# Expert products of an FNet + PEER block: all sixteen groups in seven part products, a seventh pair, sums kept or made in the expert stage

## Chip, core and metric

The kernel runs on one core of a Trainium2 chip. The core's engines work from queues of their own, in the order of the program: PE (matmuls), DVE (elementwise, one-hot building), ACT (activations, copies), POOL (elementwise), and SP, which here issues the DMAs. The metric is the device time of one execution in microseconds (us). Before the change it is 1130.89 us, the median of three runs (1129.87 to 1134.87).

## The reference

x is 1 x 2048 x 512. The output is x plus two branches of its layer norm xn: a Fourier mix (real part of a DFT over both axes) and a mixture of 4096 tiny experts.

```python
q = einsum("nd,dhc->nhc", xf, w_q)              # 32 heads, two halves of 128
s1, s2 = q1 @ k1.T, q2 @ k2.T                   # 64 keys each
# top 2 of each half, 4 candidates, top 2 of them: top_s, top_e (of 4096)
g = softmax(top_s, axis=-1)
act = gelu(einsum("nd,nhkd->nhk", xf, u[top_e]))
out_B = einsum("nhk,nhk,nhkd->nd", g, act, v[top_e])
return x + fnet(xn) + out_B
```

## The kernel before

**Stages.** Up to 431 us the kernel makes the layer norm, the folded DFT, the query scores (`s_mm`, L252), their top 2 and the routing numbers. Beside that it loads u and v and splits each into an upper and a lower f16 part (`fill_uv`, L772). From 431 us on runs the expert stage, with the 2048 tokens as 16 tiles of 128. It computes all 4096 experts for each token instead of gathering them.

**The expert stage, per token tile b.**
- z: u times x for all experts, in 16 groups of 256 experts, each product as three f16 matmuls (upper·upper, upper·lower, lower·upper), then gelu on ACT into the tile's `act`.
- g: `g_mm` (L1235) makes, for 32 tokens, a matrix of the routing weights over all experts. DVE builds one-hot matrices L (128x2048, L1246) and R (128x512, L1251, times the weight in L1254), 16 tokens at a time, in three rotating L/R buffers, and PE multiplies them into one of two PSUM buffers. Four g_mm make a tile: G(b,0) to G(b,3).
- w: `w_part` (L1259) multiplies `act` by g on DVE (L1264) and splits it into f16 parts: ACT copies the upper (L1271), DVE subtracts for the lower (L1272).
- v: `v_part` (L1294), eight v steps of twelve 512-column matmuls each, sums w times v in a PSUM bank.
- `add_x` (L1309) adds x to the Fourier rows on POOL (L1314); `finish` (L1316) adds the v sum on DVE (L1318) and stores.

**Pairs.** Tiles 2 to 13 go in six pairs through `z_pair` (L1175). For three sets of four groups (QUADS: groups 4 to 15) it uses seven part products on 128-column halves instead of eight, by a Strassen-Winograd scheme: operations 1 to 7, each 24 matmuls of 128 columns (L1168). Operations 1, 2 and 4 read blocks of u, 3, 5, 6 and 7 sums of u; 4, 5, 6 and 7 read sums of x. DVE adds the parts up (L1204, L1212, L1216) with copies on ACT between. The sums of u lie in HBM (`s_d`), made in the score stage by `sum_u` (L800), and come on chip through three rotating places (`ring_load`, L1148), four per quad and pair. The sums of x for the pair lie in HBM too (`t_d`), made in the score stage by `sum_x` (L817) on POOL and ACT, and are loaded in one 512 KB transfer (`x4`). Groups 0 to 3 go as four plain steps of 24 matmuls of 256 columns (`u_part`, L1082). The order within a pair is a list, where c is a plain step and the letter after an operation names the quad:

```python
SEQ = "1a 5a 2a 6a c 3a 1b 7a 2b 5b 4a 6b c 3b 1c 7b 2c 5c 4b 6c c 3c 7c c 4c".split()
```

Tiles 0, 1, 14 and 15 go alone, through plain steps with 128 columns.

**The order of the work.** It is written out by hand: a list of phases and a plan, which hangs pieces of work on a step number (cg) of a phase.

```python
phases = [("z", 0), ("z", 1), ("v", 0)]
for b in range(2, 14, 2):
    phases += [("z", b, b + 1), ("v", b - 1), ("v", b)]
phases += [("z", 14), ("v", 13), ("z", 15), ("v", 14), ("v", 15)]
```

So a cycle is a pair, then the v phase of the last tile of the pair before, then that of the new pair's first tile. G(b,0) and G(b,1) of a pair's first tile stand within the pair (cg 9 and 12 of 16), all its w parts in the v phase behind it, and there also G and W of the second tile, whose last g_mm, G(b+1,3), stands at the start of the next pair. Into free places the plan puts U units (`compare`, L1323: a check of the DFT tables, its operands cx come by DMA, DVE folds them in L1351 and L1357) and F units (`fit`). A scheduler may move an instruction ahead of others on its engine, but each engine's queue is then fixed.

Of the kernel before, what the change touches and what calls it, by code (L numbers as in the profile page):

```python
# [31 lines left out]
QUADS = (8, 10, 12, 14), (9, 11, 13, 15), (4, 5, 6, 7)  # L32
PAIRS = tuple(range(2, 14, 2))
# [3 lines left out]
def tile_fnet_peer(ctx, tc, x, ca, cb, c5, wt, wf, wr, wq, kt, ut, vn, out):  # L37
# [17 lines left out]
    t_d = dram.tile([NT // 2, P, 4 * D], F16, name="t_d")  # L55
# [665 lines left out]
    def part_b(safe, stS, stP, stQ, stE, xt, u_sb, cmp_p, w4):  # L721
# [50 lines left out]
        def fill_uv(which, g, at=None):  # L772
# [10 lines left out]
            if which == 0 and not safe and any(g in q for q in QUADS):  # L783
                SRAW[g] = raw
                sum_u(g, 0)
# [14 lines left out]
        def sum_u(g, part, at=None):  # L800

            qd, t = next((n, q.index(g)) for n, q in enumerate(QUADS) if g in q)
            par = [f for w, f in fills if w == 0 and any(f in q for q in QUADS)].index(g) % 2
# [12 lines left out]

        def sum_x(b, part, at=None):  # L817

            n = (0, 2, 4, 4, 7, 5)[PAIRS.index(b)]
            f, t4 = scratch(n), scratch(n + 1)  # L820
            if part == 0:
                v = xq[b // 2]
                nc.gpsimd.tensor_copy(f[:, 0:1], behind(one, at))
                nc.gpsimd.tensor_tensor(f.rearrange("p (q f) -> p q f", q=2),  # L824
                                        v[:, :, 0].rearrange("p q k n -> p q (k n)"),
                                        v[:, :, 1].rearrange("p q k n -> p q (k n)"), op=ALU.add)
                b11, b21, b12, b22 = [f[:, k * 256:k * 256 + 256] for k in range(4)]
                r = [t4[:, k * 256:k * 256 + 256] for k in range(4)]
                nc.gpsimd.tensor_tensor(r[0], b12, b11, op=ALU.subtract)
                nc.gpsimd.tensor_tensor(r[1], b22, r[0], op=ALU.subtract)  # L830
                nc.gpsimd.tensor_tensor(r[2], b22, b12, op=ALU.subtract)
                nc.gpsimd.tensor_tensor(r[3], b21, r[1], op=ALU.subtract)
                return
            split4(part - 1, t4, f.bitcast(F16)[:, 0:2 * D],
                   lambda i: t_d[b // 2, :, i * 2 * D:i * 2 * D + 2 * D], at)
# [158 lines left out]
        for (which, g), n in zip(fills, slots):  # L994
            todo[n].append(lambda at, w=which, g=g: fill_uv(w, g, at))
            todo[n - (3 if n < 119 else 1)].append(lambda at, w=which, g=g: fill_load(w, g))
            if which == 0 and not safe and any(g in q for q in QUADS):
                todo[n + 5].append(lambda at, g=g: (sum_u(g, 1, at), sum_u(g, 2)))
        if not safe:
            for n, b in zip((19, 22, 25, 106, 109, 118), PAIRS):  # L1000
# [521 lines left out]
        def G(b, k):  # L1522
            return lambda: g_mm(b, k)
# [249 lines left out]
```

## Time and profile before

| | |
|---|---|
| median of three runs | 1130.89 us |
| the profiled execution, its own time | 1132.17 us |
| its span, first to last instruction | 1130.4 us |
| busy: PE, DVE, ACT, POOL | 1114.2, 960.3, 657.5, 319.4 us |
| granted PE clock | 0.998 |

Some 1.8 us of the profiled execution's time lie around the span. Times in rows are microseconds from the span's start. A row of a timeline has the start, the duration, the engine, the line of the kernel, the operation, "output<-inputs", the tile's shape and how many instructions it stands for; behind it, in brackets, the idle time of the engine before it and what ended that. A row grouped by line has, behind the bar, the busy time in all and the mean of one in ns, then the idle time before. Matmuls overlap each other, so their durations exceed the distance between their starts.

### The profile page before, as it was taken

The page shows a single profiled execution, that of the slowest core. Times are in us where ns is not written, and L with a number is a line of the kernel's source. Part 1 is how long each engine was busy: PE and PEld are TensorE (multiplying, and loading weights), DVE is VectorE, ACT ScalarE, POOL GpSimd, SP SyncE. Part 2 cuts the span into 40 slices and gives each one's busy share as a digit, 9 for nine tenths or more (in the row PEclk, how much of TensorE's full clock was granted, in tenths as well). Part 3 has the DMA queues.
Part 4 walks back from the last instruction along what each step waited for, and adds up shares of the span by engine and source line. Part 5 has one row for each costly group of instructions (what it writes and reads, how often), then busy time and mean ns, then how long its engine had stood idle before and what let it go on. Part 6 is the DMA issues. An engine that isn't in the chain of part 4 may idle for free.

```text
span 1130.4 us, 28284 instructions
## 1 busy us (share of the span) xinstructions
PE 1114.2 (99%) x11180; PEld 724.4 (64%) x11180; DVE 960.3 (85%) x2873; ACT 657.5 (58%) x1099; POOL 319.4 (28%) x357
## 2 busy tenths in 40 slices
PE   9999999999999999999999999999999999999997
PEld 6455454544545459788588479479569569567763
DVE  7899979989889899976996896896998887889782
ACT  6557598798898465454446446445435535545552
POOL 1416896888889750000000000000010010000000
PEclk9999999999999999999999999999999999999999
DMA  9984455345353315464755755665656756575742
GB/s 274 289 207 171 162 168 197 112 154 190 105 187 103 104 50 190 157 249 143 258 216 184 239 206 199 235 218 187 226 199 215 227 199 225 190 246 167 239 150 106
DMA packets 122540, 213.10 MB, mean 189 GB/s; under 512 B 34580, under 2 KB 62107, under 8 KB 122398
## 3 DMA queue, kind: packets, MB, share of 16 engines
q1 hardware_dynamic: 122096, 211.13, 56.3%
q8 instruction: 89, 1.46, 0.5%
q14 instruction: 53, 0.43, 0.1%
q10 hardware_dynamic: 302, 0.08, 0.1%
HBM read 178.34 MB, written 27.07 MB: 182 GB/s over the span
## 4 chain that ended last, share of the span: by engine, by line
PE 50%; DVE 10%; DMA 3%; ACT 2%; POOL 2%; issue 1%; SPq 0%; DVEq 0%; ACTq 0%; POOLq 0%
PE v L1301 24%; PE z L1168 13%; PE z L1095 10%; PE g L1256 4%; DMA cx<-in_cb_dram 3%; DVE L L1246 2%; DVE vals L956 1%; DVE idx L960 1%; DVE w L1264 1%; DVE act L1272 1%; DVE cx L1351 1%; DVE R L1251 0%; DMA fit<-in_wq_dram 0%; DVE cx L1340 0%; POOL v L824 0%
## 5 line engine op out<-in xcount | busy, mean ns | idle before, releaser
L252 PE MATMUL s<-m,xq 128*128 128x512 f16 x1344 | 297.4, 379 | 1.0 <-ACT ss L952 0.5
L1301 PE MATMUL v<-v,act 128*128 128x512 f16 x1056 | 233.4, 379 | 1.0 <-DMA v<-v_d 1.0
L252 PEld LDWEIGHTS <-xq 128*128 128x128 f16 x1344 | 129.8, 98 | 152.2 <-issue 2.4
L1314 POOL TENSOR_TENSOR y<-y,xr 128x512 f32<-128x512 f32 x15 | 26.1, 1740 | 623.4 <-DMA y<-y_d 383.7
L1246 DVE TENSOR_TENSOR L<-io_lam,cmp 128x2048 f16<-128x2048 f16 x128 | 157.5, 1230 | 26.9 <-PE g L1256 26.8
L1301 PEld LDWEIGHTS <-act 128*128 128x128 f16 x1056 | 101.2, 98 | 118.7 <-issue 1.3
L1095 PE MATMUL z<-xb,u 128*128 128x128 f16 (+1 forms) x2112 | 154.3, 234 | 0.1
L1095 PEld LDWEIGHTS <-u 128*128 128x128 f16 x2112 | 141.4, 98 | 6.6 <-issue 0.2
L956 DVE MAX8 vals<-ss 128x8 f32<-128x64 f32 x896 | 133.5, 216 | 5.6 <-ACT ss L952 5.6
L1301 PE MATMUL v<-v,w 128*128 128x512 f16 x480 | 106.3, 379 | 0.1
L952 ACT ACTIVATE ss<-s,wsc 128x512 f32<-128x512 f32 x120 | 81.4, 682 | 41.2 <-PE s L252 35.1
L1377 ACT ACTIVATE cx<-cx 128x896 f32<-128x896 f32 x64 | 60.4, 944 | 72.6 <-DVE cx L1357 53.2
L1168 PEld LDWEIGHTS <-s 128*128 128x128 f16 x1656 | 94.8, 98 | 0.1
L960 DVE FIND_INDEX8 idx<-vals,ss 128x8 uint16<-128x256 f32 x224 | 93.8, 419 | 0.0
L1271 ACT ACTIVATE act<-w 128x1024 f16<-128x1024 f32 x36 | 48.3, 1357 | 68.3 <-DVE w L1264 68.0
L1301 PEld LDWEIGHTS <-w 128*128 128x128 f16 x480 | 45.9, 98 | 53.6 <-issue 0.4
L1168 PE MATMUL z<-x,s 128*128 128x128 f16 x1248 | 78.1, 219 | 0.0
L1168 PEld LDWEIGHTS <-u 128*128 128x128 f16 x1296 | 74.9, 98 | 1.8 <-issue 1.4
L1256 PEld LDWEIGHTS <-L 128*128 128x128 f16 x2048 | 60.3, 96 | 12.7 <-issue 2.1
L1351 DVE TENSOR_TENSOR cx<-cx 128x512 f32<-128x512 f32 (+2 forms) x84 | 48.4, 613 | 23.5 <-DMA cx<-in_cb_dram 23.5
L1264 DVE SCALAR_TENSOR_TENSOR w<-act,scl,g 128x1024 f32<-128x1024 f32 x44 | 55.8, 1277 | 10.3 <-ACT act L1195 10.3
L1256 PE MATMUL g<-R,L 128*128 128x32 f16 x2048 | 61.9, 176 | 1.6 <-DVE R L1254 1.5
(363 smaller groups left out, 1802.3 us busy)
## 6 DMA issues: line engine op xcount, KB each, us to landing
v<-v_d SPq DMA_DIRECT2D x67, 512.0 KB, 4.3
s<-s_d SPq DMA_DIRECT2D x59, 512.0 KB, 4.8
cx<-in_cb_dram SPq DMA_DIRECT2D x64, 448.0 KB, 4.7
w<-in_wq_dram SPq DMA_DIRECT2D x28, 512.0 KB, 6.0
fit<-in_wq_dram SPq DMA_DIRECT2D x28, 512.0 KB, 4.3
uv<-in_vn_dram SPq DMA_DIRECT2D x16, 512.0 KB, 3.5
uv<-in_ut_dram SPq DMA_DIRECT2D x16, 512.0 KB, 4.2
s_d<-v SPq DMA_DIRECT2D x24, 256.0 KB, 3.7
```

What stands on the lines that cost most here:

```text
L252: nc.tensor.matmul(ps, xt[i][:, l, kd, :], m[:, r, kd, :], start=(n == 0), stop=(n == 3 * KD - 1))
L952: nc.scalar.activation(s, ps, AF.Copy, scale=inv)
L956: nc.vector.max(vals[:, i, w, :, h], s[:, g, :])
L960: nc.vector.max_index(idx[:, i, w].rearrange("p k h -> p (k h)"), vals[:, i, w, 0:2].rearrange("p k h -> p (k h)"), s[:, w * HC:g + 1, :]. ...
L1095: nc.tensor.matmul(ps if n == 1 else ps.rearrange("p (b n) -> p b n", b=2), ug[:, l, c % 2, kd, :], xb2[:, k0, r, kd, :] if n == 1 else xb ...
L1168: nc.tensor.matmul(bank[:, t * P:(t + 1) * P], lt, rt, start=(t == k == 0 and op in "125"), stop=(t == 3 and k == 5), skip_group_check=op ...
L1246: nc.vector.tensor_tensor(L.rearrange("p t (l two) -> p t l two", two=2), io_lam.rearrange("p (l two) -> p l two", two=2).unsqueeze(1).to_ ...
L1256: nc.tensor.matmul(p[:, hf, t * NC:(t + 1) * NC], L[:, t, :], R[:, t, :], start=True, stop=True)
L1264: nc.vector.scalar_tensor_tensor(w, act[:, :, ts], fw, p.rearrange("p h (n c) -> p c (h n)", c=NC), op0=ALU.mult, op1=ALU.mult)
L1301: nc.tensor.matmul(pv, w16[:, c, :, l], v_sb[g][:, r, cc, :], start=(n + cc == 0 and k == 0), stop=(n == 15 and cc == 1 and k == 2))
L1351: nc.vector.tensor_tensor(v, v, tv[:, 0:1].to_broadcast([P, len(ix), 256]), op=o)
L1377: later.append(lambda: nc.scalar.activation(tf[:, P:], tf[:, P:], AF.Abs, accum_out=chk[:, n:n + 1]))
```

## The change

- **Quads:** groups 0 to 3 become a fourth quad, so a pair has 28 part products and no plain step. u sums for groups 0 to 3 (`u_sums`) are made on POOL and ACT late in the score stage.
- **A seventh pair:** tiles 14 and 15 go as a pair; the phases end pair (14,15), v 13, v 14, v 15.
- **Order in a pair:** a v step of the tile before (`v`) and both g_mm of the pair's first tile (`g`) stand at the end, before the last operation 4.
- **One u sum per group kept on chip:** `first_sum` loads the sum that operation 5 uses over a u block that nothing reads any more (once, in the first v phase). Three sums per quad still go through the rotating places, twelve per pair as before.
- **Sums of x in the expert stage:** `sum_x` and `t_d` are gone. `x_sums` makes them from the x tiles on POOL and ACT, in the v phase before the pair, with the buffer of an `act` tile as scratch.
- **Plan:** U units at cg 4, 8, 10 and 12 of every pair; the tail's work is distributed anew.

The core of the diff:

```diff
-QUADS = (8, 10, 12, 14), (9, 11, 13, 15), (4, 5, 6, 7)
-PAIRS = tuple(range(2, 14, 2))
+QUADS = (0, 1, 2, 3), (8, 10, 12, 14), (9, 11, 13, 15), (4, 5, 6, 7)
+PAIRS = tuple(range(2, NT, 2))
...
-            SEQ = "1a 5a 2a 6a c 3a 1b 7a 2b 5b 4a 6b c 3b 1c 7b 2c 5c 4b 6c c 3c 7c c 4c".split()
+            SEQ = ("1a 5a 2a 6a 3a 1b 7a 2b 5b 4a 6b 3b 1c 7b 2c 5c 4b 6c 3c 1d 7c 2d 5d 4c 6d 3d g 7d "
+                   "v g 4d").split()
...
+        def x_sums(b, part):
+
+            s = ACT[b].rearrange("p c n -> p (c n)")
+            f, t4 = s[:, 0:2 * D], s[:, 2 * D:4 * D]
+            if part == 0:
+                nc.gpsimd.tensor_tensor(f.rearrange("p (q f) -> p q f", q=2),
+                                        xb2[:, :, 0].rearrange("p q k n -> p q (k n)"),
+                                        xb2[:, :, 1].rearrange("p q k n -> p q (k n)"), op=ALU.add)
+                b11, b21, b12, b22 = [f[:, k * 256:k * 256 + 256] for k in range(4)]
+                r = [t4[:, k * 256:k * 256 + 256] for k in range(4)]
+                nc.gpsimd.tensor_tensor(r[0], b12, b11, op=ALU.subtract)
+                nc.gpsimd.tensor_tensor(r[1], b22, r[0], op=ALU.subtract)
+                nc.gpsimd.tensor_tensor(r[2], b22, b12, op=ALU.subtract)
+                nc.gpsimd.tensor_tensor(r[3], b21, r[1], op=ALU.subtract)
+                return
+            h, l = [x4[:, n].rearrange("p o k n -> p (o k n)") for n in range(2)]
+            nc.scalar.activation(h, t4, AF.Copy)
+            nc.gpsimd.tensor_tensor(l, t4, h, op=ALU.subtract)
...
+        def first_sum(qd):
+            for t, g in enumerate(QUADS[qd]):
+                nc.sync.dma_start(u_sb[g][:, :, 1, 0:2, :].rearrange("p l k e -> p l (k e)"),
+                                  s_d[qd, 0].rearrange("p (t l f) -> t p l f", t=4, l=2)[t])
...
             for o in SEQ:
-                if o == "c":
-                    u_part(b, next(cgs))
-                    done += 2616
+                if o == "v":
+                    v_step(b[0] - 1)
+                    done += NS[o]
+                elif o == "g":
+                    g_mm(b[0], next(gs))
+                    done += NS[o]
...
         phases = [("z", 0), ("z", 1), ("v", 0)]
-        for b in range(2, 14, 2):
+        for b in range(2, NT, 2):
             phases += [("z", b, b + 1), ("v", b - 1), ("v", b)]
-        phases += [("z", 14), ("v", 13), ("z", 15), ("v", 14), ("v", 15)]
+        phases += [("v", 15)]
...
-                if phases[n + 1][1] in PAIRS and not safe:
-                    nc.sync.dma_start(x4.rearrange("p l o k n -> p (l o k n)"), t_d[phases[n + 1][1] // 2])
...
+                if c in PAIRS and not safe:
+                    ACT[c] = act_tile(c)
+                    x_sums(c, 0)
+                    put(ph, 5, lambda c=c: x_sums(c, 1))
```

What this does to the engines' own order shows at two places. The first is DVE around the end of the pair of tiles 4 and 5. Before the change, L0 to L2 and R0 to R2 are the three L/R buffers, cmp4 the routing numbers of tile 4, z5_4_2 the bank of the last quad, and the last row is the first w of tile 4:

```order
L1246 TENSOR_TENSOR L1_5726<-io_lam_72,cmp4_8227 128x2048
L1251 TENSOR_TENSOR R1_5727<-io_c_73,cmp4_8227 128x512
L1246 TENSOR_TENSOR L2_5728<-io_lam_72,cmp4_8227 128x2048
L1212 TENSOR_TENSOR w4_126<-z5_4_2_8923,w4_126 128x4x128
L1254 TENSOR_TENSOR R1_5727<-R1_5727,cmp4_8227 128x512
L1251 TENSOR_TENSOR R2_5729<-io_c_73,cmp4_8227 128x512
L1254 TENSOR_TENSOR R2_5729<-R2_5729,cmp4_8227 128x512
L1216 TENSOR_TENSOR w4_126<-w4_126,act4_8366 128x4x128
L1264 SCALAR_TENSOR_TENSOR w4_0_9205<-act4_8366,scl_93,g4_0_8877 128x1024
```

The same place of the changed kernel, whose lines are numbered 23 higher:

```order
L1235 TENSOR_TENSOR w4_125<-z5_4_3_9102,w4_125 128x4x128
L1269 TENSOR_TENSOR L2_5655<-io_lam_71,cmp4_8303 128x2048
L1274 TENSOR_TENSOR R2_5656<-io_c_72,cmp4_8303 128x512
L1269 TENSOR_TENSOR L0_5651<-io_lam_71,cmp4_8303 128x2048
L1239 TENSOR_TENSOR w4_125<-w4_125,act4_8158 128x4x128
L1277 TENSOR_TENSOR R2_5656<-R2_5656,cmp4_8303 128x512
L1274 TENSOR_TENSOR R0_5652<-io_c_72,cmp4_8303 128x512
L1277 TENSOR_TENSOR R0_5652<-R0_5652,cmp4_8303 128x512
L1269 TENSOR_TENSOR L1_5653<-io_lam_71,cmp4_8303 128x2048
L1274 TENSOR_TENSOR R1_5654<-io_c_72,cmp4_8303 128x512
L1269 TENSOR_TENSOR L2_5655<-io_lam_71,cmp4_8303 128x2048
L1277 TENSOR_TENSOR R1_5654<-R1_5654,cmp4_8303 128x512
```

Right behind this piece follows the first w of tile 4. More L and R now stand between the last quad's additions and the first w, since both g_mm of tile 4 moved to the pair's end, and the second R2, which was ahead of the first w, comes after it.

The second place is POOL from the v phase of tile 4 to that of tile 7. Before, POOL has there only the additions of `add_x`, y being the Fourier rows and xr the rows of x:

```order
L1314 TENSOR_TENSOR y3_9422<-y3_9422,xr3_9424 128x512
L1314 TENSOR_TENSOR y4_9697<-y4_9697,xr4_9699 128x512
L1314 TENSOR_TENSOR y5_10762<-y5_10762,xr5_10764 128x512
L1314 TENSOR_TENSOR y6_11036<-y6_11036,xr6_11038 128x512
L1314 TENSOR_TENSOR y7_12107<-y7_12107,xr7_12109 128x512
```

Now the sums for tiles 8 and 9 stand between, with an `act` buffer (w4) as scratch and x4 as the result:

```order
L1337 TENSOR_TENSOR y4_9859<-y4_9859,xr4_9861 128x512
L1337 TENSOR_TENSOR y5_11007<-y5_11007,xr5_11009 128x512
L1097 TENSOR_TENSOR w4_125<-xb2_99 128x1024
L1102 TENSOR_TENSOR w4_125<-w4_125 128x256
L1103 TENSOR_TENSOR w4_125<-w4_125 128x256
L1104 TENSOR_TENSOR w4_125<-w4_125 128x256
L1105 TENSOR_TENSOR w4_125<-w4_125 128x256
L1109 TENSOR_TENSOR x4_5671<-w4_125,x4_5671 128x1024
L1337 TENSOR_TENSOR y6_11287<-y6_11287,xr6_11289 128x512
```

Six POOL instructions per pair moved here from the score stage, into the v phase of the pair's first tile.

120 lines of the change are left out of this document (69 added, 51 removed).

## The prediction

> **What bounds the kernel now.** I read the windows first: busy time of each engine, stage by stage. The columns are the stretch in us, its length, then busy time of PE, PEld, DVE, ACT and POOL, the granted clock, the DMA share and GB/s.
>
> ```profile
> 0.00:431.30 431.30, 425.31 (x2700) 225.47 (x2701) 390.24 (x1887) 319.98 (x550) 292.34 (x340) 1.00 0.52 162
> 431.30:488.90 57.60, 57.28 (x884) 45.29 (x884) 54.73 (x79) 26.41 (x33) 1.27 (x1) 1.00 0.61 207
> 488.90:574.90 86.00, 85.65 (x1017) 61.80 (x1015) 65.91 (x130) 40.90 (x69) 3.97 (x2) 1.00 0.59 204
> 574.90:661.40 86.50, 86.50 (x1055) 62.77 (x1052) 71.42 (x111) 42.43 (x70) 4.15 (x2) 1.00 0.62 216
> ...
> 923.20:1009.80 86.60, 85.60 (x1022) 61.78 (x1018) 71.20 (x118) 44.04 (x74) 3.75 (x2) 1.00 0.62 215
> 1009.80:1057.80 48.00, 47.70 (x678) 35.84 (x677) 46.28 (x79) 23.68 (x38) 2.12 (x1) 1.00 0.58 192
> 1057.80:1080.80 23.00, 23.00 (x449) 22.95 (x447) 14.18 (x35) 15.01 (x29) 1.28 (x1) 1.00 0.51 165
> 1080.80:1130.40 49.60, 43.10 (x256) 20.17 (x254) 26.42 (x74) 17.33 (x30) 1.00 (x2) 0.96 0.45 146
> ```
>
> From 488.9 to 1009.8 run six equal cycles, each a z pair and two v phases; (1009.8 - 488.9) / 6 = 86.8 us each. PE is busy all through one, DVE 66 to 71 us of those shown. POOL, with two additions per cycle, is nearly idle there, while in the first 431 us it works for 292. So the matrix engine sets the time, and a saved PE microsecond counts, but only where DVE can follow. The second look is therefore the place where DVE is tightest, the stretch between the end of one pair and the start of the next. First PE's timeline (start, duration, engine, line): the last operation of the pair (4, 5), the first v matmuls, and the end of the stretch.
>
> ```profile
> 578.91 1.50 PE L1168 MATMUL z<-x,s 128*128 128x128 f16 x24
> 580.25 2.78 PE L1095 MATMUL z<-xb,u 128*128 128x256 f16 x24
> 582.87 0.95 PE L1256 MATMUL g<-R,L 128*128 128x32 f16 x32
> ...
> 614.57 1.50 PE L1168 MATMUL z<-x,u 128*128 128x128 f16 x24
> 615.91 2.75 PE L1301 MATMUL v<-v,act 128*128 128x512 f16 x12
> 618.50 0.95 PE L1256 MATMUL g<-R,L 128*128 128x32 f16 x32
> ...
> 660.56 0.95 PE L1256 MATMUL g<-R,L 128*128 128x32 f16 x32
> 661.36 1.50 PE L1168 MATMUL z<-xb,u 128*128 128x128 f16 x24
> ```
>
> Matmuls are pipelined, so I price them from start to start: a part product costs 580.25 - 578.91 = 1.34, a plain step 2.62, a v step (12 matmuls) 2.59, a g_mm 0.80. Now DVE in the same stretch, in its order: the first w row, the waits with what ended them, the second half's w rows, and the last R row.
>
> ```profile
> 616.89 2.47 DVE L1264 SCALAR_TENSOR_TENSOR w<-act,scl,g 128x1024 f32<-128x1024 f32 x2 [2.57 <-ACT act L1195]
> 619.60 1.35 DVE L1272 TENSOR_TENSOR act<-w,act 128x1024 f16<-128x1024 f32 x1 [0.23 <-ACT act L1271]
> ...
> 638.63 0.29 DVE L1332 TENSOR_REDUCE sums<-cx 128x1 f32<-128x128 f32 x1 [0.67 <-DMA cx<-in_ca_dram]
> ...
> 639.75 1.03 DVE L1351 TENSOR_TENSOR cx<-cx 128x512 f32<-128x512 f32 x2 [0.50 <-DMA cx<-in_cb_dram]
> ...
> 644.01 1.23 DVE L1246 TENSOR_TENSOR L<-io_lam,cmp 128x2048 f16<-128x2048 f16 x1 [2.37 <-PE g L1256]
> ...
> 648.17 2.35 DVE L1272 TENSOR_TENSOR w<-w,w 128x1024 f16<-128x1024 f32 x1
> ...
> 654.63 1.30 DVE L1272 TENSOR_TENSOR w<-w,w 128x1024 f16<-128x1024 f32 x1
> ...
> 659.55 0.42 DVE L1254 TENSOR_TENSOR R<-R,cmp 128x512 f16<-128x512 f16 x1
> ```
>
> DVE can begin w only when the pair's last gelu is done (616.89, 1.0 after PE's last part product), and must deliver the last R by 659.97, for a g_mm that PE starts at 660.56 and whose second half starts 0.4 later. So 43.1 us of DVE stand against 44.65 us of PE, with 1 us to spare at the end. Inside the 43.1 DVE waits 2.37 for L buffers, which is PE being late, and 1.4 for ACT and DMA.
>
> **The change part by part.** *Part products.* A pair goes from 21 part products and 4 plain steps, 21 x 1.34 + 4 x 2.62 = 38.6, to 28 x 1.34 = 37.5: -1.1 per pair, -6.6 for six. Tiles 14 and 15 went alone, 384 matmuls of 128 columns each at 1.34 / 24: 42.9 for both; as a pair 37.5, so -5.4. PE loses 12 us of work in all. Each extra quad adds three DVE additions inside the pair (0.72 each in the L1204 row below); these are hidden, since DVE has 86.5 - 71.4 = 15 us idle per cycle and most of that lies in the pair. Free slots for ACT's copies between operations shrink from four to two, 2.7 us; I take 0 for that, with 1 us per pair as the upper end.
>
> *v step and g_mm at the end of the pair.* One v step of the previous tile and both g_mm of the next now stand before the last part product. PE's work does not change, but the stretch after the pair loses a v step: 44.65 - 2.6 = 42.05 us of PE up to the same g_mm. DVE's rows in that stretch stay what they were, plus one R pair that no longer fits before the first w; the w rows start 1.3 instead of 1.0 after the pair. So DVE needs 43.1 - 2.37 (the L wait vanishes when DVE is the late one) - 0.6 (half of the other waits, an estimate) + 0.3 = 40.4, starting 1.3 late: done at 41.7, against 42.05 + 0.4 on PE. Without anything else the cycle would stay PE's: 42.5 (28 part products, a v step, three g_mm) + 42.9 = 85.4. Slack is 0.8.
>
> *Sums of x in the expert stage.* They leave the score stage and come to POOL in the v phase before each pair, inside that stretch: one 1024-wide addition, four of 256 columns, and one 1024-wide subtraction. Their rows before, grouped by line:
>
> ```profile
> L824 POOL TENSOR_TENSOR v<-xq 128x1024 f32<-128x1024 f16 x6 | 12.7, 2121 | 0.4
> L829 POOL TENSOR_TENSOR v<-v 128x256 f32<-128x256 f32 x6 | 4.4, 728 | 0.5
> L795 POOL TENSOR_TENSOR v<-v,v 128x1024 f16<-128x1024 f32 x18 | 38.4, 2133 | 5.5 <-ACT v L794 5.5
> ```
>
> That is 2.12 + 4 x 0.73 + 2.13 = 7.2 us of POOL per pair. PE reads the result only a pair later, so POOL's own time is covered. What is not covered is DVE beside it. POOL's only work there before is the y addition; three of them, from POOL's timeline, and the DVE row that overlapped each (the 647.61 one is beside the L1272 row of 648.17 above), with a normal R row ahead:
>
> ```profile
> 454.70 0.42 DVE L1254 TENSOR_TENSOR R<-R,cmp 128x512 f16<-128x512 f16 x1
> 455.33 1.27 POOL L1314 TENSOR_TENSOR y<-y,xr 128x512 f32<-128x512 f32 x1 [33.95 <-DMA zt<-z_d]
> 455.50 1.39 DVE L1254 TENSOR_TENSOR R<-R,cmp 128x512 f16<-128x512 f16 x1
> 647.61 1.74 POOL L1314 TENSOR_TENSOR y<-y,xr 128x512 f32<-128x512 f32 x1 [65.33 <-DMA y<-y_d]
> 753.24 2.26 POOL L1314 TENSOR_TENSOR y<-y,xr 128x512 f32<-128x512 f32 x1 [18.51 <-DMA y<-y_d]
> 754.25 0.72 DVE L1204 TENSOR_TENSOR w<-z,w 128x512 f32<-128x512 f32 x1
> 754.85 0.94 DVE L1251 TENSOR_TENSOR R<-io_c,cmp 128x512 f16<-128x512 f16 x1
> ```
>
> DVE lost 1.39 - 0.42 = 0.97, 2.35 - 1.30 = 1.05, and 0.94 - 0.42 = 0.52 (the row that reads PSUM, L1204, lost nothing): 0.85 per POOL operation of 1.27, or 0.67 per us of POOL. 7.2 x 0.67 = 4.8; I let 0.5 of it fall into the waits that DVE keeps and take **4.3**. The bounds are 0 (a POOL that finds only rows that read PSUM) and 7.2 (every microsecond blocks). The Trainium skill ("SBUF — State Buffer", Who interferes with whom) says the two engines share a port pair as an exclusive lock: a DVE instruction with two SBUF inputs and a POOL instruction that reads SBUF do not overlap, the second fully blocks. The rows agree in kind, for the row with a PSUM input was untouched; by that rule nearly the full 7.2 would be lost.
>
> Then DVE ends at 41.7 + 4.3 = 46.0 after the pair, and PE's last half g_mm (0.4) follows: 42.5 + 46.0 + 0.4 = **88.9** against 86.8: +2.1 per cycle, +12.6 for six. Between the bounds: 85.4 and 91.8.
>
> *First v phase.* The window from 431.3 has DVE at 95%, and the same sums for tiles 2 and 3 come there: +2 (0 to 5). Sixteen loads that put one u sum per group on chip go out on SP's queue there too, ahead of later y and cx loads; they are needed only for the pair: 0 (to 2).
>
> *Tail.* From 1009.8 PE has 5.4 us less. But in the stretch 1009.8 to 1057.8 DVE is 96% busy, and tiles 14 and 15 now need their w in two v phases after one pair, where the work was spread beside two z phases of one tile; I estimate that DVE gives back 3.4 of it: -2 (-6 to +3).
>
> *Score stage.* POOL loses six times 7.2 us and gains four times as much for the u sums of groups 0 to 3; PE is busy 425 of 431 us with other work: 0 (-1 to +1). SP loses twelve stores and six loads, nobody waits for them: 0.
>
> The sum is 12.6 + 2 - 2 = +12.6. The profiled execution has a span of 1130.4 and took 1132.17, so the changed kernel would take 1144.8 in such a run. The profiled run is 1.3 above the median, 1130.89; against that the forecast is **1143.5 us**.
>
> **The rivals.** *PE keeps the lead (faster).* If POOL costs DVE under 0.8 us per cycle, DVE still meets PE and the six cycles go at 85.4: 6 x -1.4 = -8.4, with -2 to -5.4 in the tail: 1130.9 - 12 = about **1119**. For it: the waits of 2.37 and 1.4 that DVE has today, DVE idle for 15 us per cycle, and POOL additions that got longer themselves (1.74 and 2.26 against 1.27), so that some of the price may be POOL's. Against it: all three overlaps cost DVE at least 0.5. The sign turns where POOL costs 2.2 per cycle, 0.3 per us.
>
> *The gain is eaten and no more (same).* POOL costs 1.5 to 3: cycles between 86.2 and 87.6, so -4 to +5 with the tail's -2: 1125 to 1136, say **1131**. For it: DVE's checks (cx rows) have no consumer on PE and could be run later by then.
>
> *Full blocking (slower still).* POOL's 7.2 all count: 91.8 per cycle, 6 x 5.0 = 30, +5 in the first v phase, -2: **1164**; with four fifths of DVE's rows liable, 5.8, 90.4: 1130.9 + 21.6 + 2 - 2 = 1152. The skill's lock rule, where it holds to the letter, gives this one.
>
> **How the numbers follow.** The forecast with its surroundings (1137 to 1149) gets 0.46, PE in the lead 0.23, the gain just eaten 0.17, full blocking 0.14. To leave out no more than 2 in 10, the range reaches down to most of the PE case, 1119, and up to where four fifths of the rows block, 1152. Cases of both signs hold much of the chance; the likeliest one's own range is 1137 to 1149. A difference of 0.5%, 5.7 us, is about what a measurement here can tell from none: faster 0.24, within it 0.17, slower 0.59.
>
> **What would show it.** In the changed profile the pair should take 42.5 us on PE with no gap; the L wait in the stretch after the pair should be gone; the last g_mm before a pair should wait for DVE's R by 3 to 4 us per cycle; DVE rows beside x sums should be longer by 4 to 5 us in sum; PE's busy time should fall by 12 us while the span grows. It is wrong if PE stays without waits in the cycles (then 85.4), if the DVE rows beside POOL are no longer than elsewhere, or if the pair itself stretches, by a copy or a sum from HBM that comes late.

## The result and the profile after

The changed kernel takes 1212.29 us (median of six runs, 1203.61 to 1216.18), the kernel before 1132.54 in the same comparison: ratio 1.0697, 95% interval 1.0656 to 1.0737. It is slower, as forecast, but by 80 us, where the prediction had 12.6 and a range up to 1152. The profiled execution took 1211.23 us with a span of 1209.3.

The same windows as before, cut at the starts of the pairs of the changed kernel (columns as in the prediction: stretch, length, busy time of PE, PEld, DVE, ACT, POOL, granted clock, DMA share, GB/s):

```profile
0.00:431.30 431.30, 407.17 (x2423) 208.88 (x2424) 368.00 (x1782) 303.79 (x519) 272.03 (x320) 0.98 0.50 159
...
439.80:515.49 75.69, 71.53 (x1116) 58.40 (x1114) 67.62 (x129) 33.84 (x42) 11.66 (x7) 0.98 0.57 180
515.49:610.97 95.48, 87.28 (x1089) 63.74 (x1088) 74.18 (x137) 46.44 (x74) 13.25 (x8) 0.98 0.56 185
610.97:704.17 93.20, 87.68 (x1128) 64.29 (x1124) 77.84 (x117) 46.88 (x75) 14.36 (x8) 0.98 0.60 201
...
990.05:1086.70 96.65, 88.85 (x1126) 65.14 (x1123) 77.42 (x125) 48.78 (x79) 16.78 (x8) 0.96 0.57 193
1086.70:1209.30 122.60, 110.20 (x1255) 74.36 (x1250) 86.77 (x173) 52.66 (x87) 5.83 (x5) 0.98 0.50 161
```

The 79 us between the spans lie in four places. The first z matmul comes at 439.35 instead of 417.67: **+21.7**. From there to the first pair it is 76.1 instead of 71.0: **+5.1**. The six cycles take (1086.7 - 515.5) / 6 = 95.2 instead of 87.0, counted from the first matmul of each pair in both kernels: **+49**. The rest is 122.6 instead of 119.6: **+3**. The clock, 1.00 nearly everywhere before, is 0.96 to 0.98 in every one of these rows.

What PE waited for, before and after (microseconds in all, times, the longest):

```profile
...
PE g L1256 <- DVE R L1254: 1.5, 3, 1.0
...
PE v L1301 <- DMA v<-v_d: 1.0, 1, 1.0
...
PE s L252 <- ACT ss L952: 0.5, 1, 0.5
PE z L1168 <- ACT w L1215: 0.4, 1, 0.4
```

```profile
PE g L1279 <- DVE R L1277: 22.9, 20, 4.1
PE s L251 <- ACT ss L931: 19.8, 5, 9.9
PE z L1188 <- ACT act L1230: 13.4, 3, 5.3
PE z L1188 <- ACT w L1230: 6.6, 2, 3.8
PE v L1324 <- DMA v<-v_d: 4.4, 4, 1.7
PE z L1188 <- ACT act L1238: 2.3, 2, 2.1
```

The first row is the wait that the prediction spoke of; 17.8 of its 22.9 us lie in the six cycles, 3.0 per cycle. The other two large ones, on ACT in the score stage and on ACT inside the pairs, it had at nothing.

**The score stage.** ACT's own waits between 300 and 431 us, longest first, then its timeline:

```profile
ACT w L1126 <- POOL w L1123: 30.4, 4, 12.5
```

```profile
344.11 0.67 ACT L931 ACTIVATE ss<-s,wsc 128x512 f32<-128x512 f32 x1
357.30 1.06 ACT L1126 ACTIVATE w<-w 128x1024 f16<-128x1024 f32 x1 [12.52 <-POOL w L1123]
358.26 0.67 ACT L931 ACTIVATE ss<-s,wsc 128x512 f32<-128x512 f32 x1
```

L1126 is the copy that makes the upper part of a u sum of groups 0 to 3, and L931 the copy of the scores out of PSUM that PE needs. The first stood 12.5 us at the head of ACT's queue, because POOL had its sum among other work, and the score copies behind it stood as long. PE waited up to 9.9 us for one (the second row above).

**Inside a pair.** The pair of tiles 4 and 5, which starts at 610.97: SP, POOL, ACT and PE, one fence each.

```profile
614.18 0.33 SPq L1334 DMA_DIRECT2D y<-y_d  x1
616.38 1.19 SPq L915 DMA_TRANSPOSE zt<-z_d  x1
621.19 0.33 SPq L1336 DMA_DIRECT2D xr<-in_x_dram  x1
...
622.52 0.42 SPq L1451 DMA_DIRECT2D fit<-in_wq_dram  x1
```

```profile
617.60 3.57 POOL L1337 TENSOR_TENSOR y<-y,xr 128x512 f32<-128x512 f32 x1 [22.01 <-DVE act L1227]
```

```profile
628.94 1.06 ACT L1452 ACTIVATE fit<-fit 128x1024 f32<-128x1024 f32 x1 [3.47 <-DMA fit<-in_wq_dram]
...
630.00 0.58 ACT L1230 ACTIVATE act<-z 128x512 f32<-128x512 f32 x1
```

```profile
625.33 1.51 PE L1188 MATMUL z<-x,s 128*128 128x128 f16 x24
630.63 2.72 PE L1188 MATMUL z<-xb,s 128*128 128x128 f16 x24 [3.78 <-ACT act L1230]
633.14 1.84 PE L1188 MATMUL z<-xb,u 128*128 128x128 f16 x24
```

This is a chain through four queues. SP waits until POOL has added y and xr (617.60 + 3.57 = 621.17; the same addition took 1.27 at 455.33 in the kernel before), since the next xr goes into the same buffer; behind it in SP's queue stands the load of a fit unit (622.52), which lands 6.4 us later; ACT waits for that load (3.47); behind it in ACT's queue stands the copy of operation 5's bank (L1230); and PE needs this bank for operation 3. PE stood for 3.8 us, and the two operations after the gap took 2.51 and 1.67 us from start to start (the third starts at 634.81) instead of 1.34; the granted clock between 630 and 635 is 0.66. Such a gap in front of operation 3, behind a late copy at L1230, is in five of the seven pairs.

### The profile page after: what moved, and what is told of

Its sections match the earlier page's. It is cut to its first block, busy times and chain, and to the rows that moved or that the text cites. A ratio compares the mean times of both kernels' runs of the same rounds, so it can differ in the third digit from the quotient of the medians.

```text
span 1209.3 us, 29100 instructions
## 1 busy us (share of the span) xinstructions
PE 1127.0 (93%) x11516; PEld 732.9 (61%) x11516; DVE 1003.1 (83%) x2903; ACT 678.5 (56%) x1108; POOL 380.8 (31%) x381
## 4 chain that ended last, share of the span: by engine, by line
PE 27%; DVE 27%; DMA 7%; POOL 6%; issue 4%; ACT 3%; SPq 1%; POOLq 0%; DVEq 0%; ACTq 0%
PE z L1188 13%; DVE L L1269 7%; PE v L1324 5%; PE s L251 4%; DVE w L1287 4%; PE z L1070 4%; DVE act L1295 3%; DVE R L1274 2%; DVE R L1277 2%; DVE cx L1374 2%; DMA fit<-in_wq_dram 2%; DMA cx<-in_cb_dram 2%; POOL y L1337 1%; PE g L1279 1%; DVE w L1295 1%
## 5 line engine op out<-in xcount | busy, mean ns | idle before, releaser
L251 PE MATMUL s<-m,xq 128*128 128x512 f16 x1344 | 301.7, 382 | 20.3 <-ACT ss L931 19.8
L1269 DVE TENSOR_TENSOR L<-io_lam,cmp 128x2048 f16<-128x2048 f16 x128 | 162.5, 1270 | 6.8 <-PE g L1279 6.6
L1188 PEld LDWEIGHTS <-u 128*128 128x128 f16 x2688 | 158.3, 100 | 3.3 <-issue 3.1
L1188 PEld LDWEIGHTS <-s 128*128 128x128 f16 x1944 | 116.9, 101 | 22.4 <-issue 15.4
L1337 POOL TENSOR_TENSOR y<-y,xr 128x512 f32<-128x512 f32 x15 | 34.1, 2272 | 259.4 <-DMA y<-y_d 203.2
L931 ACT ACTIVATE ss<-s,wsc 128x512 f32<-128x512 f32 x120 | 80.8, 680 | 42.5 <-PE s L251 38.8
L1188 PE MATMUL z<-xb,u 128*128 128x128 f16 x1344 | 89.3, 226 | 0.0
L1279 PE MATMUL g<-R,L 128*128 128x32 f16 x2048 | 64.8, 176 | 23.2 <-DVE R L1277 22.9
L1097 POOL TENSOR_TENSOR act<-xb 128x1024 f32<-128x1024 f16 x4 | 12.5, 3120 | 230.3 <-PE v L1324 113.3
L1188 PE MATMUL z<-x,u 128*128 128x128 f16 x1344 | 82.2, 220 | 2.7 <-ACT act L1238 2.3
L1188 PE MATMUL z<-x,s 128*128 128x128 f16 x1296 | 82.4, 221 | 1.1 <-DMA s<-s_d 1.0
L1218 ACT ACTIVATE act<-act,scl 128x512 f32<-128x512 f32 x56 | 40.1, 719 | 45.5 <-DVE act L1239 23.9
```

What stands on the lines that cost most here:

```text
L251: nc.tensor.matmul(ps, xt[i][:, l, kd, :], m[:, r, kd, :], start=(n == 0), stop=(n == 3 * KD - 1))
L931: nc.scalar.activation(s, ps, AF.Copy, scale=inv)
L1188: nc.tensor.matmul(bank[:, t * P:(t + 1) * P], lt, rt, start=(t == k == 0 and op in "125"), stop=(t == 3 and k == 5), skip_group_check=op ...
L1269: nc.vector.tensor_tensor(L.rearrange("p t (l two) -> p t l two", two=2), io_lam.rearrange("p (l two) -> p l two", two=2).unsqueeze(1).to_ ...
L1279: nc.tensor.matmul(p[:, hf, t * NC:(t + 1) * NC], L[:, t, :], R[:, t, :], start=True, stop=True)
```

## The experiments

My theory after seeing the two traces had three parts: ACT's queue blocked by the u sums in the score stage, ACT's queue blocked by check units (compare or fit) in the pairs, and DVE late in the stretch after the pair because of POOL, as predicted. All times are medians, and each ratio is against the kernel before on the same chip (1131.6 to 1133.7). What is read from a trace belongs to one execution of the run.

**1. The copy of the u sums on POOL instead of ACT.**

```diff
-            nc.scalar.activation(h, s4, AF.Copy)
+            nc.gpsimd.tensor_copy(h, s4)
```

> The upper part of the u sums of groups 0 to 3 (four copies of 128x1024) is made on POOL instead of ACT; all else as in the changed kernel (1212.3). Theory: in the score stage ACT stood up to 12.5 us at the head of its queue, waiting for POOL, with the copies of the scores behind it, and PE waited 19.8 us for those. Then the first z matmul comes at about 418 to 421 us instead of 439.4, PE's wait for the scores is under 3 us, and the time is 1186 to 1195. Rival: POOL itself has too much work there and the splits of u come late whoever copies; then PE's wait stays over 10 us and the time is 1203 or more.

1204.9 us, ratio 1.0639 (1.0610 to 1.0668). The first z matmul came at 435.6, PE still waited 15.7 us for the scores. The rival had more of it: ACT then waits for POOL's sums of the other groups (L811) and for its routing operations (L869), which stand behind the added ones.

```profile
372.44 1.15 ACT L793 ACTIVATE v<-v,ss 128x1024 f16<-128x1024 f32 x1 [10.23 <-POOL v L811]
...
401.66 0.26 ACT L872 ACTIVATE c<-c 128x64 f32<-128x64 f32 x1 [18.52 <-POOL c L869]
```

**2. The fit unit of each pair moved to the v phase behind it.**

```diff
-                    for cg in (8,):
-                        put(ph, cg, F[0])
+                    put(("v", ph[1]) if ph[1] < 14 else ("v", 15), 0, F[0])
```

> The fit unit at step 8 of every pair (one 512 KB load and one ACT operation) is put at the start of the v phase behind it; all else as in the changed kernel (1212.3). Theory: within the pair ACT waits for the load of the fit unit, the copy of operation 5 stands behind that, and PE waits 2.8 to 5.3 us, after which the clock is low for some us. Then these waits (20.0 us in six of seven pairs) fall under 5 us and the time is 1180 to 1192. Rival: SP's queue, held up by the y addition, is late with the sums of u as well; then PE waits for these loads instead, and the time is 1202 or more.

1205.8 us, 1.0643 (1.0617 to 1.0669): a miss for both, since the time is the rival's and its cause is not. The waits for L1230, which were in five pairs and not six, fell from 20.0 to 6.0 us, but those for the copies of operations 6 and 7 (L1232, L1238) rose from 3.3 to 15.1. It was not SP's sums (1.9 us). Something else now stood in ACT's way.

**3. The sums of x made for the first pair only.**

```diff
+                    if c == 2:
-                    x_sums(c, 0)
+                        x_sums(c, 0)
```

> The sums of x are made for the first pair only; later pairs use the same ones, so their part products are of the wrong data but of the same size. This leaves out six POOL and one ACT operation in each of six v phases; all else as in the changed kernel (1212.3). Theory, as in the prediction: POOL beside DVE costs 4.3 us per cycle; PE's waits for R, 17.7 us in the six cycles, fall under 6, the lower clock behind them goes too, and the time is 1186 to 1200. Rival: the waits for R come from the shorter stretch after the pair; then they stay over 12 and the time is 1206 or more.

1187.1 us, 1.0480 (1.0446 to 1.0513): the theory; the waits for R in the six cycles fell from 17.8 to 5.9. The sums over the six cycles, of the changed kernel and of this run (PE, PEld, DVE, ACT, POOL busy):

```profile
sum 571.21, PE 529.61 PEld 387.18 DVE 472.32 ACT 282.98 POOL 86.99; mean PE 88.27 PEld 64.53 DVE 78.72 ACT 47.16 POOL 14.50
```

```profile
sum 546.28, PE 520.44 PEld 380.07 DVE 444.59 ACT 276.16 POOL 26.22; mean PE 86.74 PEld 63.34 DVE 74.10 ACT 46.03 POOL 4.37
```

DVE does the same work in both, and needs 472.3 - 444.6 = 27.7 us less, 4.6 per cycle. It lost this where the prediction said: without the sums the R rows, whose inputs are all in SBUF, fall from 0.51 (L1274, L1277, mean) to 0.42 and 0.45, while rows that read PSUM stay at 0.69 (L1227) and 1.28 (L1287). POOL is busy 60.8 us less, of which 58.3 are the six sets, 9.7 each where a set had 7.2 in the score stage; the other 2.5 are y additions that got shorter. The cost is on both sides.

**4. Both g_mm and the v step back to their places.**

```diff
-            SEQ = ("1a 5a 2a 6a 3a 1b 7a 2b 5b 4a 6b 3b 1c 7b 2c 5c 4b 6c 3c 1d 7c 2d 5d 4c 6d 3d g 7d "
-                   "v g 4d").split()
+            SEQ = ("1a 5a 2a 6a 3a 1b 7a 2b 5b 4a 6b 3b 1c 7b 2c 5c 4b 6c g 3c 1d 7c 2d 5d 4c g 6d 3d 7d "
+                   "4d").split()
```

> Within the pair both g_mm stand between the third and fourth quad again and the v step is back in the v phase; all else as in the changed kernel (1212.3). Theory, as in the prediction: the stretch after the pair has 2.6 us more of PE for the same DVE work, so the waits for R fall by 1.5 to 2.5 per cycle and the time is 1196 to 1205. Rival: DVE is late because of POOL whatever the order; the waits for R change by under 0.7 per cycle, the time is 1207 to 1217.

1201.5 us, 1.0604 (1.0578 to 1.0630): the theory. In the profiled execution, the fastest of five (1193.7), the waits for R fell from 22.9 to 13.6 us, in the six cycles from 17.8 to 7.0, 1.8 per cycle.

**5. The u sums of groups 0 to 3 in the middle of the score stage,** by the code of the other groups (`sum_u`, behind each split).

```diff
-            if which == 0 and not safe and g > 3:
+            if which == 0 and not safe:
                 SRAW[g] = raw
                 sum_u(g, 0)
```

> The u sums of groups 0 to 3 are made where those of the other groups are, right behind each group's split in the middle of the score stage, by the same code, not in its last 85 us; all else as in the changed kernel (1212.3). Theory: the 7.2 us per group hurt only because they came in one block at 346 to 395 us, ahead of the splits and routing on POOL's queue and of the score copies on ACT's; at 100 to 300 us POOL has room since the sums of x left it. Then PE waits under 3 us for the scores, the first z matmul comes at 417 to 422 us instead of 439.4, and the time is 1185 to 1194. Rival: POOL is short of time in the score stage as a whole; the waits move to another place, over 10 us stay and the time is 1203 or more.

1189.8 us, 1.0503 (1.0482 to 1.0525): the theory. The first z matmul is at 416.9, and PE no longer waits for score copies. The sums cost 22.5 us at 346 to 395 us and nothing that the time shows at 145 to 205. Two more things differ there: the copies on ACT come some steps later in the order instead of right behind the sums, and POOL has 8.5 of 28.6 us less to do, since `sum_u` reads u before it is split and needs no 1024-wide addition (L1117).

**6. Number 5, and the sums of x in the score stage too,** with a seventh set, stored and loaded as before.

```diff
-                    x_sums(c, 0)
-                    put(ph, 5, lambda c=c: x_sums(c, 1))
+                    nc.sync.dma_start(x4.rearrange("p l o k n -> p (l o k n)"), t_d[c // 2])
```

> As the run with the earlier u sums, and the sums of x are made in the score stage as in the kernel before (a seventh set added for tiles 14 and 15), stored, and loaded in one transfer per pair; nothing of them on POOL in the expert stage. Theory: the gains add up, 20 us in the score stage and 25 in the cycles: 1160 to 1172. Rival: with both, POOL is full in the score stage and the first z matmul is late by 8 us or more: 1175 or more.

1168.1 us, 1.0319 (1.0270 to 1.0368): the theory's range; the cycles average 90.6. But the first z matmul is at 426.1, so POOL, now with all sums, costs the score stage 9 us again; PE waits 5.6 of them for it.

**7 and 8. Number 6 with the fit unit moved (edit 2), and that with the order back (edit 4).**

> As the run with all sums early, and the fit unit of every pair in the v phase behind it. Theory: the small waits for ACT's copies of operations 3, 6 and 7 that stayed when the fit unit alone was moved (3 us per pair) come from DVE, which is late with the w parts and additions because of POOL; without x sums they go too: waits in a pair under 1.5 us, time 1135 to 1147. Rival: with no plain step between them the copies are too close by themselves; 2 us or more per pair stay, and the time is 1150 to 1162.

> As the run with sums and fit moved, and both g_mm between the third and fourth quad, the v step back in the v phase. Theory: without POOL beside it DVE meets PE in the stretch after the pair (slack 0.8 us by the prediction's working), so the order makes under 5 us, below or above. Rival: the stretch is short of DVE even so, and the order back gains 6 to 12 us.

1167.5 us (1.0299, 1.0281 to 1.0317) and 1166.0 (1.0290, 1.0272 to 1.0308). For the first both expectations were too low, the theory by 20 us: with no x sums near, the copies of operations 6 and 7 were still late. For the second the theory holds, 1.4 us: without POOL's sums the stretch after the pair has room, and the order hardly matters.

**9. Number 8 without the four compare units in each pair.**

```diff
                     for cg in (4, 8, 10, 12):
-                        put(ph, cg, U)
```

> As the run with sums and fit moved and the order back (1166.0), and the four compare units in each pair are left out: 28 of the 68 tests of the DFT tables aren't made (their cells are set to zero), nothing else is. Theory: what is left in a pair, 3 us of waits per cycle for ACT's copies of operations 6, 7 and 5, comes from the compare units' ACT operation at the head of ACT's queue, which waits for DVE and DMA with these copies behind it; these waits fall under 1 us per cycle, the cycles from 90.2 to 87 or less, the time is 1140 to 1150. Rival: the copies are too close by themselves, with two operations between where there was a plain step; 2 us or more stay, and the time is 1156 or more.

1144.8 us, 1.0105 (1.0071 to 1.0139): the theory, 21 us less. Of its six cycles the first, the third, the fifth and the last:

```profile
503.86:590.49 86.63, 85.03 (x1089) 61.97 (x1088) 60.85 (x113) 41.78 (x65) 3.24 (x2) 1.00 0.60 197
...
677.20:763.35 86.15, 85.69 (x1128) 62.70 (x1125) 68.77 (x105) 42.63 (x66) 3.52 (x2) 1.00 0.59 199
...
849.48:935.62 86.14, 85.68 (x1127) 62.69 (x1124) 69.13 (x103) 43.05 (x66) 3.68 (x2) 1.00 0.60 199
935.62:1025.67 90.05, 86.33 (x1128) 62.80 (x1125) 71.67 (x119) 44.06 (x68) 2.83 (x2) 1.00 0.57 192
```

So the seven-product pair with four quads can run at the speed of PE, at full clock and without a plain step; the prediction's PE sum was 85.4. It doesn't in every cycle: in the last one PE waits 2.6 us for R, and the six together take 521.8 us, as much as in the kernel before (522.1).

**10. Number 8 with the seventh set of sums of x 31 steps later.**

```diff
-            for n, b in zip((19, 22, 25, 106, 109, 118, 33), PAIRS):
+            for n, b in zip((19, 22, 25, 106, 109, 118, 64), PAIRS):
```

> As the run with sums and fit moved and the order back (1166.0), and the sums of x for tiles 14 and 15, the set that the kernel before doesn't have, come 31 steps later in the score stage. Theory: the 8 us by which the first z matmul is late there (425.8 against 417 to 418) are PE's two waits for POOL at 173 and 183 us, where this set and the u sums of groups 0 to 3 meet on POOL's queue; then both are gone and the time is 1156 to 1162. Rival: the u sums alone are enough for these waits; 1163 or more.

1167.0 us, 1.0284 (1.0231 to 1.0337): the rival. The first z matmul stayed at 426.8; it is not this one set.

**11. The changed kernel with edits 2 and 9 only** (no check unit with a load in a pair).

> The changed kernel (1212.3) with the fit unit of every pair moved to the v phase behind it and the four compare units in each pair left out (28 of 68 tests of the DFT tables aren't made); order, sums of x and of u as in the changed kernel. Theory: in the changed kernel itself PE's waits within the pairs (3.2 us per cycle, and 1.5 to 2 of low clock behind each) come from check units at the head of ACT's queue; they go, and DVE has 28 units less, so the time is 1160 to 1178. Rival: with POOL's sums in place ACT's copies wait for DVE anyway; 2 us or more per cycle stay in the pairs and the time is 1190 or more.

1182.2 us, 1.0447 (1.0411 to 1.0483): a little above the theory's range, far from the rival. PE's waits in the six cycles:

```profile
PE g L1279 <- DVE R L1277: 17.9, 16, 2.4
PE z L1188 <- DMA s<-s_d: 2.0, 4, 0.7
PE v L1324 <- DMA v<-v_d: 1.6, 2, 1.0
```

Not one wait for ACT is left. The waits for R, 3.0 per cycle, are those of the changed kernel (17.8), and the cycles average 541.28 / 6 = 90.2: this is the prediction's term nearly by itself.

**12. The kernel before with the seventh pair alone** (tiles 14 and 15 in its own three-quad scheme), which brings a fourth compare unit per pair.

```diff
-PAIRS = tuple(range(2, 14, 2))
+PAIRS = tuple(range(2, NT, 2))
...
+                    for cg in (4, 9, 12, 15):
+                        put(ph, cg, U)
```

> The kernel before with only tiles 14 and 15 as a seventh pair, in its own scheme (three quads, four plain steps, order, sums in the score stage, one set of sums of x more), and a fourth compare unit per pair at step 4. Theory: 42.9 - 38.6 = 4.3 us of PE go, and the plain steps leave ACT room for the check units, so the time is 1125 to 1131. Rival: the fourth check unit per pair makes ACT's copies late here too, and the set of sums more delays the score stage: 1134 or more.

1143.3 us, 1.0094 (1.0066 to 1.0121): the rival. In the profiled execution, the slowest of six (1148.8), the cycles average 89.8, though nothing in the pairs of tiles 2 to 13 had changed but the compare unit at step 4.

**13 and 14. That with three units per pair; and the kernel before with the fourth unit and nothing else.** The edit of the second:

```diff
-                    for cg in (9, 12, 15) if len(ph) == 3 else (0, 2, 3, 6):
+                    for cg in (4, 9, 12, 15) if len(ph) == 3 else (0, 2, 3, 6):
```

> The run with the seventh pair only (1143.3), with three compare units per pair at the places of the kernel before, and the seven left over in the v phases of tiles 13 and 14. Theory: the fourth unit made ACT's copies late; without it the cycles are 86.8 as before and PE's 4.3 us at the end count: 1125 to 1131. Rival: the set of sums more, or the tail with its v phases in a row, costs as much: 1133 or more.

> The kernel before with a compare unit at step 4 of each pair added to the three there; the 68 units are then used up six places earlier. Nothing else is changed. Theory: the cycles grow by 2 to 5 us as in the seventh-pair run, by ACT's copies waiting behind it; 1142 to 1152. Rival: the cycles stay at 86.8, and what was slower there came with the seventh pair; 1130 to 1136.

1138.8 us (1.0063, 1.0045 to 1.0081): the theory for the cycles, which are back at 86.8, and the rival for the time, since PE waited 3.9 us in the tail for DVE's units there. And 1151.1 us (1.0174, 1.0149 to 1.0200), the theory: one check unit more per pair costs the kernel before 19 us. The pair of tiles 10 and 11 shows how. First the kernel before, where the pair starts at 836.03, SP, POOL and ACT:

```profile
839.42 0.33 SPq L1311 DMA_DIRECT2D y<-y_d  x1
...
844.16 0.34 SPq L1313 DMA_DIRECT2D xr<-in_x_dram  x1
...
845.03 1.08 SPq L1428 DMA_DIRECT2D fit<-in_wq_dram  x1
```

```profile
842.10 2.04 POOL L1314 TENSOR_TENSOR y<-y,xr 128x512 f32<-128x512 f32 x1 [18.22 <-DVE act L1272]
```

```profile
849.91 1.06 ACT L1429 ACTIVATE fit<-fit 128x1024 f32<-128x1024 f32 x1 [0.86 <-ACT act L1202]
```

Then with the fourth unit, where it starts at 843.95, SP, POOL, ACT and PE:

```profile
845.42 1.07 SPq L1330 DMA_DIRECT2D cx<-in_ca_dram  x1
846.55 0.43 SPq L1331 DMA_DIRECT2D cx<-in_cb_dram  x1
847.65 0.33 SPq L1311 DMA_DIRECT2D y<-y_d  x1
...
854.01 0.34 SPq L1313 DMA_DIRECT2D xr<-in_x_dram  x1
...
854.87 0.42 SPq L1428 DMA_DIRECT2D fit<-in_wq_dram  x1
```

```profile
851.72 2.26 POOL L1314 TENSOR_TENSOR y<-y,xr 128x512 f32<-128x512 f32 x1 [19.26 <-DVE cx L1351]
```

```profile
861.06 1.06 ACT L1429 ACTIVATE fit<-fit 128x1024 f32<-128x1024 f32 x1 [2.09 <-DMA fit<-in_wq_dram]
```

```profile
862.74 2.72 PE L1168 MATMUL z<-x,u 128*128 128x128 f16 x24 [3.15 <-ACT w L1215]
```

The unit's loads go out first on SP. The load of y leaves 3.7 us after the pair's start instead of 3.4, POOL's addition begins 4.1 us behind it instead of 2.7, xr and the fit load behind xr wait for that, and the fit load leaves 10.9 us after the pair's start instead of 9.0. In the kernel before ACT didn't wait for that load; the added unit made it late. It is the chain of the changed kernel, in code that the change had not touched.

**15 and 16. Number 8 with three units per pair, and number 13 with its left-over units spread** (three more on the first pair, one more on the last, one in v 14, two in v 13). In number 15 too the first pair has six and the last four.

```diff
-                    for cg in (4, 8, 10, 12):
+                    for cg in (9, 11, 12, 13, 14, 15) if ph[1] == 2 else (9, 12, 13, 15) if ph[1] == 14 else (9, 12, 15):
```

> As the run with sums and fit moved and the order back (1166.0: four quads, seven pairs, sums in the score stage), with compare units at 9, 12 and 15 of a pair, as in the kernel before, and the seven left over in the first and the last pair and the last v phases. Theory: the fourth unit made most of the waits, so the cycles fall from 90.2 to 87 or less and the time is 1142 to 1152. Rival: without plain steps three units are late as well; cycles of 88.5 or more, 1157 or more.

> As the seventh pair only with three compare units per pair (1138.8), the seven units left over spread on the first pair, the last pair and v 14. Theory: the wait of 3.9 us in the tail goes and what is left of the 4.3 us shows: 1127 to 1133. Rival: DVE has too little time in the tail without z phases of one tile; 1135 or more.

1155.6 us (1.0200, 1.0166 to 1.0234), between the two; cycles of 89.3 in the profiled execution, the slowest of four (1162.0). So about half of the 21 us that the units cost in number 8 goes with the fourth one (1166.0 to 1155.6), and the other half (to 1144.8) comes from the rest, as many per pair, but in the first and the last, as the kernel before carries with cycles of 87.0. That the plain steps hid them there is likely but not shown. And 1130.9 us, 0.9990 (0.9974 to 1.0006): with no more than three units in the middle pairs the seventh pair makes no difference that can be told from none. No version was measurably faster than the kernel before.

## Why the prediction was wrong

**PE's work: right, but it became no time.** 12 us less was forecast; cycles of 86.1 almost without waits (run 9) stand against 85.4 in the sum. The prediction's windows put the old cycle at 86.8; from pair start to pair start it is 87.0. Yet run 9's six cycles together are no shorter than before, its tail is 1.2 us shorter where 5.4 less PE work was forecast, and the seventh pair alone (run 16) changes nothing.

**Sums of x beside DVE: right.** Forecast 4.3 us of DVE per cycle, out of 7.2 of POOL. DVE lost 4.6 per cycle, and leaving them out gave 25 us. With the check units out of the way (run 11) the cycle was 90.2 and the R wait 3.0; forecast was 88.9. The Trainium skill ("SBUF — State Buffer", Who interferes with whom) says that of a DVE instruction with two SBUF inputs and a POOL instruction that reads SBUF the one that comes second is fully blocked, whichever it is. The runs agree in the sum: DVE lost 4.6 us per set and POOL 2.5, together 7.1, about the 7.2 that POOL needs alone. The prediction's full blocking case put all of it on DVE.

**The order in the pair: right.** The slack of 0.8 without POOL, none with it: putting the order back gains 10.8 us with the sums there, 1.4 without.

**First v phase and tail: small.** Forecast +2 (0 to 5), measured +5.1, with one wait for R of 4.1 us; the stretch takes 77.1 us in run 5 and 71.7 in run 6, where the sums of x are gone from it. Forecast -2 (-6 to +3), measured +3, with 6.0 us of waits, 3.8 of them for a copy at L1230 in the last pair.

**"Score stage ... 0 (-1 to +1)": wrong, this step failed first.** I took POOL's work off in sum, six sets out and four in, and looked at PE being busy. What counts is where in the stage the work stands and who waits in order behind it. Of the six sets in the kernel before, three began at 119 to 134 us and three at 364 to 399, so POOL was about as busy near the end of the stage before as after (40.3 us in 350 to 400 before, 43.4 after). But the four new sets stand there close together, at 347 to 393, ahead of splits and routing, and their copies stand on ACT right behind them, ahead of the score copies: 21.7 us late at the first z matmul, all of which went when the sums were made earlier, with their copies hung later and without the 1024-wide additions (run 5). Which of the three counts most isn't separated; taking the copies from ACT alone (run 1) brought the first z matmul 3.7 us forward. The order showed the place of the sums; I didn't go on to ask what stood behind the copies that wait for them.

**"Free slots for ACT's copies ... I take 0 ..., with 1 us per pair as the upper end": wrong.** PE waits up to 5.3 us for such a copy, 3.2 per cycle. The prediction named a late copy among its signs of being wrong, but gave it nothing beyond that 1 us. I counted the copies against each other, not the foreign instructions in the same queue, which wait for DMAs. And the fourth check unit per pair, which was in the plan of the change, is in no term of the sum; alone it costs the kernel before 19 us (run 14). Leaving out the four compare units gave 21 us (run 9), leaving them out and moving the fit unit too 30 us in the changed kernel (run 11).

**The low clock: missing.** Matmul work was 12 us less, but PE's busy time rose from 1114.2 to 1127.0, which by estimate makes some 25 us of slower clock behind the waits. It isn't a separate cause, for in the cycles where the waits went (run 9), the clock was 1.00 again; it makes each wait dearer than its own length. Behind a wait of 3.8 us the next two operations lost 1.5. The Trainium skill ("TensorE: Matmul & The Clock Gate", What's actually happening) says that an idle window of about 3.4 us brings the clock down to half and as long a busy one brings it back. The row at 630.63, behind a wait of 3.8 us, agrees, 2.51 us for an operation of 1.34; but a shorter wait can do it too (last section), and there the measurement decides.

**What it comes to.** Alone, the runs took off 22.5 us (u sums, 5), 25.2 (x sums, 3), 30.0 (check units, 11) and 10.8 (order, 4), which overlap; all together 67.5 (run 9, 1144.8, where 28 compare units are left out). Of the four only the sums of x and the order were in the prediction: the direction was forecast for a reason that the runs show, and the larger part of the 80 us came from steps that it had at nothing. The profiled execution of run 9 is 13.6 us longer than that of the kernel before: 9.5 in the score stage, where the added sums still are, and 5.6 up to the first pair, less 1.5 behind it. Of the 9.5, PE waits 5.6 for POOL; which of POOL's operations it is was not settled (run 10). In the 5.6, DVE stands 4.28 us at a row that adds up cells of the check units (L1501), ahead of an L row, and PE then waits 2.8 for R; run 8 doesn't have that row there and takes 73.1 us for this stretch, against 76.7 in run 9 and 71.0 before.

One sum among the rivals was off by 2 us: "1125 to 1136" takes the tail's -2 off its lower end and not off its upper one.

## What to carry to other kernels

When work is moved, list for every engine that touches it, DMA queues included, what stands behind it in that queue at the new place; the sum of an engine's busy time over a stage says nothing about that. Units without a consumer, such as checks, cost nothing only while nothing needed stands behind them: adding one is a change to the critical path, and so may be taking away slow steps beside them. And once PE has waits, price them with the clock that they lose.

## What the runs showed of the hardware

Two things I had not expected. A wait of 2.1 us can be enough to bring the clock down: in the first pair PE waited 2.13 us before 530.55, and that operation took 1.75 and the next 2.56 us from start to start (to 534.86) instead of 1.34, at a granted clock of 0.60. In other places a longer wait left the clock as it was: in run 6 the operation behind one of 2.91 us, at 970.39, took 1.34.

```profile
530.55 1.96 PE L1188 MATMUL z<-x,u 128*128 128x128 f16 x24 [2.13 <-ACT act L1238]
532.30 2.72 PE L1188 MATMUL z<-x,s 128*128 128x128 f16 x24
```

And POOL beside DVE's work of the expert stage slows both: its 1024-wide f16 addition took 3.12 and 2.75 us (mean, two buffers) there, and 2.12 in the score stage, in rows of the same shape. In the score stage DVE is busy too, 368 of 431 us, with other operations. That it is the rows with all inputs in SBUF that matter is what run 3 shows from DVE's side.

```profile
L1097 POOL TENSOR_TENSOR act<-xb 128x1024 f32<-128x1024 f16 x4 | 12.5, 3120 | 230.3 <-PE v L1324 113.3 <-DVE cx L1382 58.9 <-DVE cx L1380 58.1
L1097 POOL TENSOR_TENSOR w<-xb 128x1024 f32<-128x1024 f16 x3 | 8.2, 2747 | 110.4 <-PE v L1324 94.9 <-DMA xb<-xt_d 15.4
L1117 POOL TENSOR_TENSOR w<-u 128x1024 f32<-128x1024 f16 x4 | 8.5, 2124 | 0.0
```
